# Weight conversion in pairs of pieces, and pooling of batches 2 and 3 by accumulating DMAs, in a fused attention and mixture kernel

## The chip, the cores and the metric

The kernel runs on one core of one Trainium2 chip. The metric is the device time of one execution, in microseconds (us), as the median of the runs of a measurement. All times below are of the kernel before, unless said otherwise.

## What is computed

Three layers follow one another, all in float32 (cut to what matters):

```python
# attention with pooled keys and values; q, k, v are (4, 8, 576, 64)
k_p = k.reshape(B, H, S // 8, 8, D).mean(axis=3)
v_p = v.reshape(B, H, S // 8, 8, D).mean(axis=3)
attn = softmax(q @ k_p.T / sqrt(D))
x = heads_joined(attn @ v_p)                 # 2304 tokens x 512
# first dense layer; its weights arrive as float64
h = x @ w_in                                 # 512 -> 2048
x = (h * cos(h)) @ w_out                     # 2048 -> 512
# mixture of 8 experts, weighted by a Sinkhorn-normalized gate
P = sinkhorn(exp(x @ w_gate), 8 rounds)
out = sum(P[:, e:e+1] * (relu(x @ w1[e]) @ w2[e]) for e in range(8))
```

## The kernel before

The 2304 tokens are worked in six blocks of 384 (j = 0 to 5). Every float32 product that needs full precision is made of three products of rounded parts: a number is cut into a high part (a copy rounded by ScalarE) and a low part (a subtraction on VectorE or GpSimd, by `halves`).

**Attention** (`attn_weights`, `attn_values`) makes, for each block and each half of the heads, scores on TensorE (`psc`), a maximum, a subtraction, an exponential, row sums and a multiplication with the reciprocals (`at`, in `normalize`), then transposes on TensorE (`ptr`), copies of these (`pt`), and products with the pooled values (`px`), which ScalarE and VectorE cut into `xh` and `xl`. Keys and values must be pooled over eight neighbours first. Batch 0 has its own way, batch 1 is pooled by TensorE (`pk`, `pv` with `band`). For batches 2 and 3, `load_k` and `load_v` load four tiles `kr` and four tiles `vr` each, and `pool_steps` adds each tile's eight parts in three halvings (4, 2, 1 parts); each addition goes to VectorE or GpSimd, as the planner likes. Two ScalarE copies then spread `ks` into `kbd`, which the scores read.

**The first dense layer** runs in two groups of blocks (0 to 3, then 4 and 5) and in four units u of 512 hidden columns. `hidden1` makes `ph` and the cosine (`r`, then `gh` and `gl`), `output1` makes `po` and adds it into `acc`. Its weights are float64. `convert` turns one piece (512 columns) of them into two float32 parts: a 512 KB load (`raw`), an absolute value on ScalarE (`m`), five VectorE operations (L820 to L828: two on `m`, one that joins `m` with the raw words, one that makes `cw`, one that multiplies the low words into it), an addition (`cw`, VectorE or GpSimd), and the two parts `wc` by `halves`. Each part is stored to a scratch tensor `wac` in HBM and, except for u = 0 in the first group, loaded again (`cached`) when TensorE needs it. There are 8 pieces a unit, 32 in all. The pieces of u = 0 are needed within the first microseconds, while attention for blocks 0 to 2 goes on beside them.

**The mixture** takes 48 steps (16 weight units times 3 pairs of blocks); each is a Strassen product with 7 instead of 8 block products (`px`, `py`, `pv` in `first_layer`, `pc`, `qc` in `strassen_layer`).

**What sets the order.** No loop issues instructions directly. Every operation is a node of a graph, with an estimated time for its engine, the tiles it reads and writes, and a latest time (`late`) worked out backwards from goals of TensorE's nodes. `Graph.schedule` then plans: again and again, it takes on each engine the most urgent node that could start first, and emits it. A node with two engines (`VG(n)`: VectorE or GpSimd) goes where it is expected to be done, with some slack. Five queues result: TensorE (PE), ScalarE (ACT), VectorE (DVE), GpSimd (POOL) and SyncE (SP), which issues all DMAs. Each runs its nodes in this order, and an instruction whose input is late holds all that stand behind it on the same engine. Tiles have few slots, and a node that opens a tile waits for the slot. Where the plan sees TensorE idle, `keep_busy` fills in products with the identity matrix (`psc<-ident` and the like, L484), whose result nobody reads. `SHIFTS` is a table of 28 entries (first node, count, by) that moves the latest times of nodes before the planning; its nodes lie in attention, the first dense layer and the first steps of the mixture (node numbers 21 to 2937 of 7773).

Of the kernel before, what the change touches and what calls it, by code (L numbers as in the profile page):

```python
# [20 lines left out]
POOL = 8  # L21
# [31 lines left out]
SHIFTS = (  # L53
# [4 lines left out]
)  # L58
# [59 lines left out]


# [6 lines left out]
class Graph:  # L126

    SIGNAL = {"PE": 0.2, "A": 0.1, "V": 0.1, "G": 0.1, "SP": 0.0}
    HOLD = {"PE": 0.02, "A": 0.2, "V": 0.2, "G": 0.3, "SP": 0.2}

# [114 lines left out]
    def schedule(self, log=None):  # L245
# [28 lines left out]
        while left:  # L274
            best = None
            for e in names:
                found = []
                low = FAR
                for node in ready[e]:
# [7 lines left out]
                    if (e == "G" or (e == "V" and node.port)):  # L287
                        start = max(start, port)
# [104 lines left out]
def pool(n):  # L393
    return 0.24 + n * 0.0022
# [17 lines left out]
def fused_kernel(ctx: ExitStack, tc: tile.TileContext, qT, kT, vT, v0, k1, v1, wa1, wb1, wa2, wb2, wg, out):  # L412
# [33 lines left out]
    k_m, k_cw, k_cs = many(early, "cvm", 2, True), many(early, "cvw", 2, True), many(early, "cvs", 4, True)  # L446
# [110 lines left out]
    def pool_steps(how, r, out, reads_out, n_free):  # L557

        n = POOL // 2
        while n > 1:  # L560
            w = n * n_free
            h = V(w) if how == "V" else VG(w) if how == "VG" else {"engine": "G", "us": pool(w), "port": True}
            tt(h, lambda n=n: r()[:, :n], lambda n=n: r()[:, :n], lambda n=n: r()[:, n:2 * n], ALU.add, [], reads_out[:1])
            n //= 2
        h = V(n_free) if how == "V" else VG(n_free) if how == "VG" else {"engine": "G", "us": pool(n_free), "port": True}
        tt(h, out, lambda: r()[:, 0], lambda: r()[:, 1], ALU.add, reads_out[:1], reads_out[1:])
# [10 lines left out]
    def load_first_k(n, goal):  # L577

        t = buf(xtag[("xh1", "xl1")[n]], [P, 2, POOL, SP], F32, "k0")
        for i in range(2):  # L580
            load(lambda i=i: t[:, i], lambda i=i: kT[:, 0, 2 * n + i], P * POOL * SP * 4, writes=[(t, i)], goal=goal)
        return [(t, i) for i in range(2)]

    def pool_first_k(tiles):
        for hp, (t, i) in enumerate(tiles):
            pool_steps("V", lambda t=t, i=i: t[:, i], lambda t=t, i=i: t[:, i, 0], [(t, i), (t, i)], SP)
# [3 lines left out]
    def load_first_v(goal):  # L590

        tiles = []
        for tag in ("xl2", "xh3", "xl5"):
            t = buf(xtag[tag], [P, 2, DM], F32, "v0")
# [37 lines left out]

    def into_kbd(b, ks, ap, **more):
# [6 lines left out]
    def load_k(b):  # L640
# [15 lines left out]
        for hp in range(HP):  # L656
            kr = buf(k_raw, [P, POOL, SP], F32, "kr")
            load(lambda kr=kr: kr.tile, lambda hp=hp: kT[:, b, hp], P * POOL * SP * 4, writes=[kr], release=250 if b == 3 else 0.0)
            pool_steps("VG", lambda kr=kr: kr.tile, lambda hp=hp: ks[:, hp], [kr, (ks, hp)], SP)
        into_kbd(b, ks, lambda: ks.tile)  # L660

    def load_v(b):
# [4 lines left out]
        for hp in range(HP):  # L667
            vr = buf(k_raw, [SP, POOL, 2 * D], F32, "vr")
            load(lambda vr=vr: vr.tile, lambda hp=hp: vT[:, b - 1, hp], SP * POOL * 2 * D * 4, writes=[vr], release=250 if b == 3 else 0.0)
            pool_steps("VG", lambda vr=vr: vr.tile,  # L670
                       lambda hp=hp: vs[:, 2 * hp:2 * hp + 2, :].rearrange("p h d -> p (h d)"), [vr, (vs, hp)], 2 * D)
# [83 lines left out]
    def x_tiles(j):  # L755
        return tuple(buf(xtag[f"{n}{j}"], [P, KC, NB], F32R, f"{n}{j}") for n in ("xh", "xl"))

    def attn_values(j, half):
# [20 lines left out]
        for hh in range(2):  # L779
# [18 lines left out]
            activate(NB, lambda hp=hp: hi[:, hp, :], px, reads=[bank], writes=[(hi, hp)], from_psum=True)  # L798
            if (j, half) in REST_ON_PE:
                pe(0.19, lambda px=px, hp=hp: nc.tensor.matmul(  # L800
                    out=px(), lhsT=minus.tile, rhs=hi[:, hp, :], start=False, stop=True, skip_group_check=True),
                   [minus, (hi, hp)], [bank], goal=FAR)
                activate(NB, lambda hp=hp: lo[:, hp, :], px, reads=[bank], writes=[(lo, hp)], from_psum=True)
                continue
            tt(V(NB, False), lambda hp=hp: lo[:, hp, :], px,
               lambda hp=hp: hi[:, hp, :].bitcast(F32), ALU.subtract, [bank, (hi, hp)], [(lo, hp)])
# [3 lines left out]
    def convert(u, i, raw=None):  # L810

        if raw is None:
            raw = load_piece(u, i)
# [6 lines left out]
        add("V", one(FU), lambda: v.tensor_scalar(out=mf(), in0=mf(), scalar1=F64_LOW, scalar2=F64_HIGH, op0=ALU.max,  # L820
                                                  op1=ALU.min), [], [m], port=True)
        add("V", one(FU), lambda: v.tensor_scalar(out=m.tile, in0=m.tile, scalar1=3, scalar2=0x3FFFFFFF,
                                                  op0=ALU.logical_shift_left, op1=ALU.bitwise_and), [], [m], port=True)
        add("V", two(FU), lambda: v.scalar_tensor_tensor(out=m.tile, in0=high(), scalar=-2**30, in1=m.tile,
                                                         op0=ALU.bitwise_and, op1=ALU.bitwise_or), [raw], [m], port=True)
        add("V", one(FU), lambda: v.tensor_scalar(out=w.tile.bitcast(I32), in0=m.tile, scalar1=-2**23, scalar2=None,
                                                  op0=ALU.bitwise_and), [m], [w], port=True)
        add("V", two(FU), lambda: v.scalar_tensor_tensor(out=w.tile, in0=low(), scalar=2.0**-52, in1=w.tile, op0=ALU.mult,  # L828
                                                         op1=ALU.mult), [raw], [w], port=True)
        tt(VG(FU), lambda: w.tile, mf, lambda: w.tile, ALU.add, [m], [w])  # L830
        parts = [buf(k_w if u == 0 else k_cs, [P, FU], F32R, "wc") for _ in range(2)]
# [587 lines left out]
```

## Time and profile before

| what | value |
|---|---|
| median of 3 runs | 1937.77 us (1937.17 to 1937.92) |
| span of the profiled execution, first to last instruction | 1935.3 us |
| median less that span | 2.5 us |
| TensorE busy in the span | 1920.6 us (99%), 13056 products |
| VectorE, ScalarE, GpSimd busy | 1497.4, 1080.9, 385.2 us |
| granted TensorE clock | 0.999 of full speed |
| DMA traffic | 392.89 MB, 203 GB/s on average |

The profile is of one execution. Its own device time is not given apart from the span, so sums are made against the span, and the 2.5 us by which the median is longer are carried along. Products on TensorE overlap, so its busy time says that it had work, not that it ran at its peak; the waits of TensorE are what it lost entirely. Times within the span count from its first instruction.

### The profile page before, as it was taken

The numbers are of one execution on the slowest core, as the hardware profiler recorded it, in microseconds if no ns is written. First come the engines' busy times: TensorE is split into PE (matmuls) and PEld (weight loads), VectorE is DVE, ScalarE is ACT, GpSimd is POOL, SyncE is SP. The second block draws the span as 40 slices with busy tenths as digits, with TensorE's granted clock in tenths as the row PEclk, the third lists the DMA queues.
The fourth block names the chain that finished last, engine by engine and source line by source line (L and its number), as shares of the span: only waits on it lengthen the run. The fifth ranks groups of instructions, "written<-read, shape, count | busy, mean of one in ns | idle before, by whom it ended". The sixth has DMA issues, their size and how long they took to land.

```text
span 1935.3 us, 34165 instructions
## 1 busy us (share of the span) xinstructions
PE 1920.6 (99%) x13056; PEld 1887.3 (98%) x13056; DVE 1497.4 (77%) x2783; ACT 1080.9 (56%) x2318; POOL 385.2 (20%) x317
## 2 busy tenths in 40 slices
PE   9999999999999999999999999999999999999999
PEld 7799999899999999999999999999999999999998
DVE  8997887855787777777787787777777877877776
ACT  5664545743556665555556555555555565555553
POOL 2523343310102021212112021212121120212120
PEclk9999999999999999999999999999999999999999
DMA  8465566443465646546546455455465464554552
GB/s 296 143 193 183 190 219 243 164 152 104 176 226 225 230 180 238 212 180 235 211 176 261 170 229 228 185 234 211 182 234 211 176 261 169 229 227 183 227 215 112
DMA packets 102020, 392.89 MB, mean 203 GB/s; under 512 B 11360, under 2 KB 16096, under 8 KB 101856
## 3 DMA queue, kind: packets, MB, share of 16 engines
q1 hardware_dynamic: 101856, 390.71, 54.2%
q8 instruction: 103, 1.69, 0.4%
q14 instruction: 61, 0.50, 0.1%
HBM read 352.65 MB, written 38.01 MB: 202 GB/s over the span
## 4 chain that ended last, share of the span: by engine, by line
PE 96%; DVE 3%; ACT 0%; issue 0%; DMA 0%; SPq 0%; POOL 0%; DVEq 0%; POOLq 0%; ACTq 0%
PE pc L1282 21%; PE qc L1282 16%; PE py L1187 16%; PE px L1187 10%; PE pv L1187 10%; PE po L862 3%; PE po L864 3%; PE po L863 3%; PE ph L862 3%; PE ph L863 3%; PE ph L864 3%; DVE at L512 1%; PE psc L684 1%; PE px L787 1%; PE ptr L773 1%
## 5 line engine op out<-in xcount | busy, mean ns | idle before, releaser
L1282 PE MATMUL pc<-vhi,gl 128*128 128x256 f32 x1152 | 322.8, 280 | 0.0
L1282 PE MATMUL pc<-vlo,gh 128*128 128x256 f32 x1152 | 322.7, 280 | 0.0
L1282 PE MATMUL pc<-vhi,gh 128*128 128x256 f32 x1152 | 322.0, 280 | 0.0
L1187 PE MATMUL py<-xc,whi 128*128 128x384 f32 x1152 | 295.1, 337 | 0.8 <-DVE c L512 0.8
L512 DVE TENSOR_TENSOR gl<-sf,gh 128x384 fp32r<-128x384 f32 x384 | 229.9, 627 | 31.0 <-ACT gh L495 30.9
L495 ACT ACTIVATE gh<-sf 128x384 fp32r<-128x384 f32 x384 | 194.3, 522 | 92.5 <-DVE sf L512 90.4
L1282 PE MATMUL qc<-vhi,gh 128*128 128x256 f32 x864 | 243.8, 282 | 0.5 <-DVE qc L512 0.5
L512 POOL TENSOR_TENSOR raw<-raw 128x512 f32<-128x512 f32 x44 | 57.2, 1301 | 938.0 <-DVE wlo L512 530.9
L1282 PE MATMUL qc<-vhi,gl 128*128 128x256 f32 x864 | 242.4, 281 | 0.0
L1282 PE MATMUL qc<-vlo,gh 128*128 128x256 f32 x864 | 241.5, 279 | 0.0
L1282 PEld LDWEIGHTS pc<-vhi,gl 128*128 128x128 f32 x1152 | 216.7, 188 | 0.0
L1282 PEld LDWEIGHTS pc<-vhi,gh 128*128 128x128 f32 x1152 | 216.4, 188 | 0.0
L1282 PEld LDWEIGHTS pc<-vlo,gh 128*128 128x128 f32 x1152 | 216.4, 188 | 0.0
L1187 PEld LDWEIGHTS py<-xc,whi 128*128 128x128 f32 x1152 | 200.6, 188 | 1.8 <-DVE c L512 1.1
L1187 PE MATMUL px<-xc,whi 128*128 128x384 f32 x768 | 197.7, 338 | 0.0
L1187 PE MATMUL pv<-xc,whi 128*128 128x384 f32 x768 | 196.7, 337 | 0.0
L1187 PE MATMUL py<-xc,wlo 128*128 128x384 f32 x576 | 193.7, 336 | 0.0
L1282 PEld LDWEIGHTS qc<-vhi,gh 128*128 128x128 f32 x864 | 162.3, 188 | 2.5 <-DVE qc L512 0.9
L1282 PEld LDWEIGHTS qc<-vlo,gh 128*128 128x128 f32 x864 | 162.4, 188 | 0.0
L1282 PEld LDWEIGHTS qc<-vhi,gl 128*128 128x128 f32 x864 | 162.3, 188 | 0.0
L862 PE MATMUL ph<-xh,wc 128*128 128x384 f32 x384 | 132.3, 345 | 1.5 <-DVE r L512 1.5
L862 PE MATMUL po<-gh,wc 128*128 128x384 f32 x384 | 132.5, 345 | 0.0
(173 smaller groups left out, 4619.0 us busy)
## 6 DMA issues: line engine op xcount, KB each, us to landing
xc<-xc SPq DMA_DIRECT2D x350, 768.0 KB, 6.7
wc<-wac SPq DMA_DIRECT2D x112, 256.0 KB, 3.6
raw<-wa SPq DMA_DIRECT2D x48, 512.0 KB, 4.8
raw<-wb SPq DMA_DIRECT2D x48, 512.0 KB, 7.0
wac<-wc SPq DMA_DIRECT2D x64, 256.0 KB, 3.1
out<-acc SPq DMA_DIRECT2D x18, 256.0 KB, 2.0
qc<-qt SPq DMA_DIRECT2D x30, 128.0 KB, 4.0
kr<-kt SPq DMA_DIRECT2D x8, 288.0 KB, 5.0
```

The costliest lines, as they stand in the source:

```text
L495: lambda: nc.scalar.activation(out=out(), in_=in_(), func=func, **{k: v() if callable(v) else v for k, v in more.items()}),
L512: (nc.gpsimd if e == "G" else nc.vector).tensor_tensor(out=out(), in0=in0(), in1=in1(), op=op)
L684: nc.tensor.matmul(out=ps[off:off + n, 2 * hh:2 * hh + 2, :].rearrange("p h s -> p (h s)"), lhsT=qc()[:, hh, off:off + n], rhs=kpool_at[b] ...
L773: nc.tensor.transpose(ps[:, h, :], at[:, i, h, :], ident.tile)
L787: nc.tensor.matmul(out=bank[e * D:(e + 1) * D, off:off + n], lhsT=vs[b][:, 2 * hp + e, :], rhs=pt[:, 2 * hh + e, off:off + n], start=(off ...
L862: nc.tensor.matmul(out=ps, lhsT=lh, rhs=rh, start=(i == 0), stop=False)
L863: nc.tensor.matmul(out=ps, lhsT=lh, rhs=rl, start=False, stop=False)
L864: nc.tensor.matmul(out=ps, lhsT=ll, rhs=rh, start=False, stop=(i == total - 1))
L1187: nc.tensor.matmul(out=ps(), lhsT=l[:, k], rhs=r[:, c, :], start=(start and c + n == 0), stop=(c + n == 3), skip_group_check=True)
L1282: nc.tensor.matmul(out=ps, lhsT=l[:, r], rhs=m[:, k], start=(start and h + n == 0), stop=(h + n == 3), skip_group_check=True)
```

## The change

It has four parts.

1. `convert` works on a pair of pieces: one load of 1 MB, and the operations on 1024 columns, so that 32 chains become 16. For u = 0 the two pieces of a pair are still cut apart into four tiles `wc`. For u = 1 to 3 the parts are written in place, the high one over `m`, the low one over `cw`, and stored by two DMAs of 512 KB; the four tiles kept for parts go away. The two raw slots are now the later places of blocks 4 and 5 of `x` (`Half`).
2. Batches 2 and 3 are pooled by `summed`: SP loads parts 0 and 1 of all heads into one tile `part`, three DMAs issued by GpSimd add the parts 2 and 3, 4 and 5, 6 and 7 into it, and one addition joins the two halves. The inputs are laid out for that on the host side of the interface (`ks`, `vs`).
3. The planner's model: consecutive VectorE and ScalarE instructions are taken to overlap by 0.08 and 0.1 us, GpSimd's DMAs are given a time to landing and 0.9 us of GpSimd, and are taken not to hold the port that VectorE and GpSimd share; nodes that issue such DMAs become urgent 7 us earlier.
4. `SHIFTS` is empty.

```diff
-SHIFTS = (
-    (1245, 20, -1.1), (2934, 4, -1.3), (185, 2, -1.4), (2725, 4, 2.0), (2209, 8, -0.6), (560, 8, -8.3), (91, 4, 1.3),
...
-)
+SHIFTS = ()
...
+    OVERLAP = {"PE": 0.0, "A": 0.1, "V": 0.08, "G": 0.0, "SP": 0.0}
...
-            if node.engine == ("SP",) and node.size:
-                node.late -= 3.0
+            if node.size:
+                node.late -= 3.0 if node.engine == ("SP",) else 7.0
...
-            free[e] = end
+            free[e] = end - self.OVERLAP[e]
...
-            if e == "G" or (e == "V" and node.port):
+            if e == "G" and not node.size or (e == "V" and node.port):
                 port = end
-            if node.size:
+            if node.size and e == "G":
+                dma = max(dma, start + 0.8) + node.size / 300e3
+                end = max(dma, start + 4.0) + 1.5
+            elif node.size:
                 dma = max(dma, start + 0.8) + node.size / 300e3
                 end = dma + 1.5
...
-                s.est = max(s.est, end + (0.0 if same else self.SIGNAL[e] + s.pad))
+                s.est = max(s.est, end + (0.35 * self.OVERLAP[e] if same else self.SIGNAL[e] + s.pad))
...
+    def summed(rows, n, src, out, writes, release=0.0):
+
+        t = buf(k_raw, [rows, 2, n], F32, "part")
+        load(lambda: t.tile, lambda: src()[:, :2], rows * 2 * n * 4, writes=[t], release=release)
+        for j in range(2, POOL, 2):
+            add("G", 0.9, lambda j=j: nc.gpsimd.dma_start(out=t.tile, in_=src()[:, j:j + 2], accum_op=ALU.add), [], [t],
+                size=rows * 4 * n * 4)
+        tt(VG(n), out, lambda: t[:, 0], lambda: t[:, 1], ALU.add, [t], writes)
...
-        for hp in range(HP):
-            kr = buf(k_raw, [P, POOL, SP], F32, "kr")
-            load(lambda kr=kr: kr.tile, lambda hp=hp: kT[:, b, hp], P * POOL * SP * 4, writes=[kr], release=250 if b == 3 else 0.0)
-            pool_steps("VG", lambda kr=kr: kr.tile, lambda hp=hp: ks[:, hp], [kr, (ks, hp)], SP)
+        summed(P, HP * SP, lambda: kS[:, b - 2], lambda: ks.tile.rearrange("p h s -> p (h s)"), [ks], 250.0 if b == 3 else 0.0)
         into_kbd(b, ks, lambda: ks.tile)
...
-        m, w = buf(k_m, [P, FU], I32, "m"), buf(k_cw, [P, FU], F32, "cw")
+        m, w = buf(k_m, [P, 2 * FU], I32, "m"), buf(k_cw, [P, 2 * FU], F32, "cw")
...
-        activate(FU, mf, lambda: high().bitcast(F32), AF.Abs, reads=[raw], writes=[m])
+        activate(2 * FU, mf, lambda: high().bitcast(F32), AF.Abs, reads=[raw], writes=[m])
...
+        if u:
+            t = [lambda: m.tile.bitcast(F32R), lambda: w.tile.bitcast(F32R)]
+            activate(2 * FU, t[0], lambda: w.tile, reads=[w], writes=[m])
+            tt(VG(2 * FU), t[1], lambda: w.tile, lambda: t[0]().bitcast(F32), ALU.subtract, [m], [w])
...
-    FIRST = "kqKqqQQQffvff"
+    FIRST = "kqKqqQQQfvf"
```

How the order moves, at three places. A row gives the line in the kernel, the operation, and the tiles out<-in with the shape.

VectorE at the start, where attention of block 0 is normalized (`sm`, `rs`, then `at<-at,rs`) before its transposes. Before:

```order
L512 TENSOR_TENSOR at<-psc,mx 128x288 x2
L820 TENSOR_SCALAR m<-m 128x512
L822 TENSOR_SCALAR m<-m 128x512
L824 SCALAR_TENSOR_TENSOR m<-raw_186,m 128x512
L703 TENSOR_SCALAR sm_230<-sm_230 128x4
L705 RECIPROCAL rs<-sm_277 128x4
L750 TENSOR_REDUCE sm<-at 128x12
L703 TENSOR_SCALAR sm<-sm 128x12
L705 RECIPROCAL rs<-sm 128x12
L512 TENSOR_TENSOR at<-at,rs 128x288
```

With the change:

```order
L527 TENSOR_TENSOR at<-psc,mx 128x288 x2
L717 TENSOR_SCALAR sm_228<-sm_228 128x4
L719 RECIPROCAL rs<-sm_257 128x4
L527 TENSOR_TENSOR at<-at,rs 128x288
L717 TENSOR_SCALAR sm_269<-sm_269 128x4
L719 RECIPROCAL rs<-sm_269 128x4
L527 TENSOR_TENSOR at<-at,rs 128x288
L837 TENSOR_SCALAR m<-m 128x1024
L839 TENSOR_SCALAR m<-m 128x1024
L841 SCALAR_TENSOR_TENSOR m<-raw_181,m 128x1024
```

The multiplications now stand ahead of the first conversion, and the sum over the second half of the heads (`sm<-at 128x12`) behind it.

GpSimd, where batch 2 is pooled. Before:

```order
L512 TENSOR_TENSOR ks<-kr 128x72
L512 TENSOR_TENSOR gl<-r,gh 128x384 x3
L512 TENSOR_TENSOR kr<-kr 128x288 x2
L512 TENSOR_TENSOR gl<-r,gh 128x384 x2
L512 TENSOR_TENSOR kr<-kr 128x144 x2
L512 TENSOR_TENSOR ks<-kr 128x72 x2
L512 TENSOR_TENSOR vr<-vr 72x512
L512 TENSOR_TENSOR vr<-vr 72x256
L512 TENSOR_TENSOR vs<-vr 72x128
```

With the change:

```order
L527 TENSOR_TENSOR gl<-r,gh 128x384 x2
L650 DMA part<-ks 128x576
L650 DMA part<-vs 72x1024
L650 DMA part<-ks 128x576
L650 DMA part<-vs 72x1024
L650 DMA part<-ks 128x576
L650 DMA part<-vs 72x1024
L527 TENSOR_TENSOR gl<-r,gh 128x384
L527 TENSOR_TENSOR cw<-m,cw 128x1024
L527 TENSOR_TENSOR ks<-part 128x288
L527 TENSOR_TENSOR vs<-part 72x512
```

Additions between the `gl` operations become six DMA issues in a row, the third and the later ones each waiting for the DMA before it on its tile; `gl` and the conversion stand behind them.

ScalarE, where `kbd` of batch 2 is filled (the scores of block 3 read it). Before:

```order
L495 ACTIVATE at<-at 128x864
L503 ACTIVATE acc<-po 128x384
L495 ACTIVATE kbd_154<-ks 64x4x72 x2
L503 ACTIVATE acc<-po 128x384
L495 ACTIVATE at<-at 128x864
```

With the change:

```order
L510 ACTIVATE m<-cw 128x1024
L518 ACTIVATE acc<-po 128x384
L510 ACTIVATE kbd_151<-ks 64x4x72
L510 ACTIVATE r<-ph 128x384
L510 ACTIVATE kbd_151<-ks 64x4x72
L510 ACTIVATE gh<-r 128x384
```

The copies now have the evacuation of a hidden bank (`r<-ph`) directly behind the first of them.

## Rows read from the trace of the kernel before

**Rows 1.** The page: span, busy time of each engine, chain that ended last.

```profile
span 1935.3 us, 34165 instructions
...
PE 1920.6 (99%) x13056; PEld 1887.3 (98%) x13056; DVE 1497.4 (77%) x2783; ACT 1080.9 (56%) x2318; POOL 385.2 (20%) x317
...
PE 96%; DVE 3%; ACT 0%; issue 0%; DMA 0%; SPq 0%; POOL 0%; DVEq 0%; POOLq 0%; ACTq 0%
```

**Rows 2.** Busy time by stretch: start:end, length, busy (xcount) of each engine.

```profile
13.50:80.30 66.80, 62.31 (x403) 49.70 (x404) 63.15 (x124) 42.52 (x82) 28.19 (x30) 1.00 0.73 242
58.00:76.00 18.00, 14.02 (x84) 12.91 (x83) 16.88 (x29) 10.76 (x21) 9.05 (x10) 1.00 0.54 176
76.00:125.00 49.00, 48.87 (x298) 42.41 (x297) 47.71 (x96) 34.03 (x61) 18.27 (x17) 1.00 0.45 144
125.00:350.00 225.00, 225.00 (x1322) 220.73 (x1321) 186.19 (x334) 117.96 (x224) 80.06 (x72) 1.00 0.61 207
530.00:1930.00 1400.00, 1399.73 (x9965) 1397.66 (x9963) 1081.24 (x2014) 790.47 (x1750) 226.03 (x165) 1.00 0.54 209
```

**Rows 3.** Waits of PE over the span: what waited for whom, us, times, longest.

```profile
PE ph L484 <- ACT r L495: 1.7, 1, 1.7
PE ph L862 <- DVE r L512: 1.5, 1, 1.5
PE psc L484 <- DVE at L512: 1.5, 1, 1.5
PE py L1187 <- DVE c L512: 0.8, 1, 0.8
PE po L864 <- DVE wc L512: 0.8, 1, 0.8
PE ptr L773 <- DVE sm L703: 0.7, 1, 0.7
```

**Rows 4.** Timeline of PE: start, us, engine, line, operation, tiles, count, idle before.

```profile
13.64 4.51 PE L484 MATMUL psc<-ident 128*128 128x128 f32 x38 [1.52 <-DVE at L512]
17.99 0.60 PE L773 MATMUL ptr<-ident,at 128*72 128x128 f32 x4
...
66.57 1.38 PE L484 MATMUL ph<-ident 128*128 128x128 f32 x10 [1.66 <-ACT r L495]
...
81.16 1.19 PE L773 MATMUL ptr<-ident,at 128*72 128x128 f32 x8
```

**Rows 5.** Timeline of DVE, the same columns.

```profile
13.51 0.42 DVE L820 TENSOR_SCALAR m<-m 128x512 f32<-128x512 f32 x1
...
14.42 0.69 DVE L824 SCALAR_TENSOR_TENSOR m<-raw,m 128x512 int32<-128x512 int32 x1
...
17.07 0.40 DVE L512 TENSOR_TENSOR at<-at,rs 128x288 f32<-128x288 f32 x1
...
25.50 0.56 DVE L512 TENSOR_TENSOR xl<-px,xh 128x384 fp32r<-128x384 f32 x1 [0.65 <-ACT xh L495]
...
80.36 1.30 DVE L512 TENSOR_TENSOR at<-at,rs 128x288 f32<-128x288 f32 x2
...
83.42 3.78 DVE L512 TENSOR_TENSOR at<-at,rs 128x288 f32<-128x288 f32 x3
```

**Rows 6.** Timeline of POOL, the same columns.

```profile
20.20 1.51 POOL L512 TENSOR_TENSOR wc<-cw,wc 128x512 fp32r<-128x512 f32 x1 [3.34 <-ACT wc L495]
...
32.58 1.27 POOL L512 TENSOR_TENSOR cw<-m,cw 128x512 f32<-128x512 f32 x1 [5.04 <-DVE cw L828]
...
82.66 4.22 POOL L512 TENSOR_TENSOR vr<-vr 72x512 f32<-72x512 f32 x3
```

**Rows 7.** Timeline of ACT, the same columns.

```profile
76.97 0.89 ACT L495 ACTIVATE kbd<-ks 64x288 f32<-64x288 f32 x2
```

**Rows 8.** DMA issues: tiles, queue, operation, count, KB each, median us to landing.

```profile
raw<-wb SPq DMA_DIRECT2D x48, 512.0 KB, 7.0
kr<-kt SPq DMA_DIRECT2D x8, 288.0 KB, 5.0
```

More of the change, by code (lines that the diff above doesn't have):

```diff
@@ L117, in __getitem__, with part, __init__ @@
         return self.tile[key]
+    def part(self, n):
+        return self, n
+class Half:
+    def __init__(self, buf, k):
+        self.buf, self.k = buf, k
+    def __getitem__(self, key):
+        return self.buf.tile[:, self.k][key]
+    def part(self, n):
+        return self.buf, (self.k, n)
 class Node:
@@ L411, in fused_kernel @@
 @with_exitstack
[L412 removed]
+def fused_kernel(ctx: ExitStack, tc: tile.TileContext, qT, kT, kS, vS, v0, k1, v1, wa1, wb1, wa2, wb2, wg, out):
     nc = tc.nc
@@ L666, in load_v @@
         vs = buf(k_vs, [SP, H, D], F32, "vs")
[L667 to L671, printed above, removed]
+        summed(SP, DM, lambda: vS[:, b - 2], lambda: vs.tile.rearrange("p h d -> p (h d)"), [vs], 250.0 if b == 3 else 0.0)
         vpool[b] = vs
@@ L824, in convert @@
[L824 to L829, printed above, removed]
@@ L830, in convert @@
-        tt(VG(FU), lambda: w.tile, mf, lambda: w.tile, ALU.add, [m], [w])
-        parts = [buf(k_w if u == 0 else k_cs, [P, FU], F32R, "wc") for _ in range(2)]
-        halves(FU, lambda: w.tile, w, lambda k: parts[k].tile, parts)
-        for k in range(2):
-            load(lambda k=k: wac[u, i, k], lambda k=k: parts[k].tile.bitcast(F32), P * FU * 4, reads=[parts[k]],
-                 writes=[kept_wa[u, i, k]])
-        return parts
+        activate(2 * FU, mf, lambda: high().bitcast(F32), AF.Abs, reads=[raw], writes=[m])
@@ new lines, in convert @@
+        add("V", one(2 * FU), lambda: v.tensor_scalar(out=mf(), in0=mf(), scalar1=F64_LOW, scalar2=F64_HIGH, op0=ALU.max,
+                                                      op1=ALU.min), [], [m], port=True)
+        add("V", one(2 * FU), lambda: v.tensor_scalar(out=m.tile, in0=m.tile, scalar1=3, scalar2=0x3FFFFFFF,
+                                                      op0=ALU.logical_shift_left, op1=ALU.bitwise_and), [], [m], port=True)
+        add("V", two(2 * FU), lambda: v.scalar_tensor_tensor(out=m.tile, in0=high(), scalar=-2**30, in1=m.tile,
+                                                             op0=ALU.bitwise_and, op1=ALU.bitwise_or), [raw], [m], port=True)
@@ new lines, in convert @@
+        add("V", one(2 * FU), lambda: v.tensor_scalar(out=w.tile.bitcast(I32), in0=m.tile, scalar1=-2**23, scalar2=None,
+                                                      op0=ALU.bitwise_and), [m], [w], port=True)
+        add("V", two(2 * FU), lambda: v.scalar_tensor_tensor(out=w.tile, in0=low(), scalar=2.0**-52, in1=w.tile, op0=ALU.mult,
+                                                             op1=ALU.mult), [raw], [w], port=True)
+        tt(VG(2 * FU), lambda: w.tile, mf, lambda: w.tile, ALU.add, [m], [w])
@@ new lines, in convert @@
+        pieces = (2 * n, 2 * n + 1)
+        if u:
+            t = [lambda: m.tile.bitcast(F32R), lambda: w.tile.bitcast(F32R)]
+            activate(2 * FU, t[0], lambda: w.tile, reads=[w], writes=[m])
+            tt(VG(2 * FU), t[1], lambda: w.tile, lambda: t[0]().bitcast(F32), ALU.subtract, [m], [w])
+            for k, b in enumerate((m, w)):
+                load(lambda k=k: wac[u, 2 * n:2 * n + 2, k].rearrange("i p n -> p i n"),
+                     lambda b=b: b.tile.bitcast(F32).rearrange("p (i n) -> p i n", i=2), P * 2 * FU * 4, reads=[b],
+                     writes=[kept_wa[u, i, k] for i in pieces])
+            return None
@@ new lines, in convert @@
+        out = []
+        for c, i in enumerate(pieces):
+            parts = [buf(k_w, [P, FU], F32R, "wc") for _ in range(2)]
+            halves(FU, lambda c=c: w[:, c * FU:(c + 1) * FU], w, lambda k, parts=parts: parts[k].tile, parts)
+            for k in range(2):
+                load(lambda i=i, k=k: wac[u, i, k], lambda k=k, parts=parts: parts[k].tile.bitcast(F32), P * FU * 4, reads=[parts[k]],
+                     writes=[kept_wa[u, i, k]])
+            out.append(parts)
+        return out
@@ L948, in fused_kernel @@
                 if u == 0:
-                    for i in range(2 * FC):
-                        weights[i] = convert(0, i, raws[i] if i < len(raws) else None)
-                else:
-                    for i in range(2 * FC):
-                        convert(u, i)
+                    for n in range(FC):
+                        weights[2 * n], weights[2 * n + 1] = convert(0, n, raws[n] if n < len(raws) else None)
+                else:
+                    for n in range(FC):
+                        convert(u, n)
                     for i in range(2 * FC):
```

71 lines of the change are left out of this document (35 added, 36 removed), and 3 rows, old and new, of the table SHIFTS.

## The prediction

> **What bounds the kernel now.** I read the page first, then a table of stretches, then the waits of TensorE, and last the timelines around those waits.
>
> The page [rows 1] says that TensorE is busy for 1920.6 of 1935.3 us and that 96% of the chain that ended last is its own work. The change takes none of that work away: both orders hold the same products, apart from products with the identity matrix, of which 25 instead of 35 are issued. So only the time that TensorE loses can be won, and that is little. The stretches [rows 2] show where: from 125 to 350 us and from 530 to 1930 us TensorE is busy all the time but for 0.3 us, between 76 and 125 us it lacks 0.13 us, and between 58 and 76 us it lacks 4 us of 18. The list of its waits [rows 3] gives the causes: 1.5, 1.7, 1.5 and 0.8 us before 76 us, where VectorE or ScalarE was late, 0.7 us at transposes in the attention of the last blocks, and 0.8 us where the mixture begins. Some time is hidden in identity products: 38 records ran from 13.64 to 17.99 us, ahead of the first transposes, and 10 from 66.57 us [rows 4]. So up to 76 us the work ahead of TensorE sets the time; after that TensorE does.
>
> Who is late there? From 13.5 to 80.3 us VectorE was busy for 63.15 of 66.8 us [rows 2]; it is the bound of the first 80 us. Part of that busy time is no work: a multiplication triple took 3.78 us while GpSimd's pooling `vr` ran for 4.22 us [rows 5, 6], though one multiplication takes 0.40 us [rows 5], so 2.6 us were waiting for the other engine.
>
> **The change, step by step.** I take one place of TensorE's program as the mark: the first transposes of block 2, which began at 81.16 us [rows 4]. In both orders the same work stands ahead of it: 96 products of `hidden1`, 45 of `output1`, 48 transposes, 28 of `px`, 20 of `pk`, 10 of `pv`, and 38 instead of 40 of scores. Whoever comes to the mark earlier ends earlier by as much, since almost nothing was lost behind it [rows 2].
>
> *Start.* Before, three conversion operations and a sum over a whole half stood between the last subtraction and the last multiplication that the first transposes need; the conversions began at 13.51 us, that multiplication at 17.07 us [rows 5]. Now the multiplications come first: about 1.4 us of small operations and two multiplications of 0.40 us, and the transposes can start near 15.0 us instead of 17.99 us [rows 4]. This is no gain by itself, since VectorE begins its conversions 1.4 us later, at 14.9 us. The first weight part was complete at 21.7 us before (20.20 plus 1.51) [rows 6]; now it takes five operations at 1024 columns (4.5 us), an addition on GpSimd (1.27 us at 512 columns [rows 6], some 2.5 us at twice that), 0.6 us on ScalarE and 1.3 us on GpSimd, so about 24 us. The order has TensorE's first hidden products near 24 us too, ahead of the pooling of batch 1, so I cost that at nothing beyond the order.
>
> *VectorE's list up to the mark.* The two queues hold these instructions from the first conversion to the multiplication that the mark waits for. Before: 8 pieces, 24 operations of one input at 0.43 us from start to start, 16 of two inputs at 0.67, 11 additions and subtractions at 0.61 [rows 5]: 27.7 us; with 90 others 59.6 us. Now: 5 pairs, two of whose pieces are already of u = 1. The trace has no such width. By 128x384 at 0.56 and 128x512 at 0.69 us [rows 5] a two-input operation gains 1 ns a column, so 1.2 us at 1024; a one-input one lies between 0.42 us (nothing more) and 0.84 us (double), and I take 0.71, since the instruction's fixed part is paid once. So 15 at 0.71, 10 at 1.2, two additions at 1.14 and four at 0.61: 27.4 us, with 78 others 57.9 us. VectorE's list is 1.7 us shorter, 1.4 us of which its later begin takes back: 0.3 us.
>
> *VectorE's blocked time.* Before, it took from 13.51 to 81.66 us (80.36 plus 1.30) [rows 5] for 59.6 us of work, so 8.5 us were spent blocked or idle, beside 28.19 us of GpSimd's work [rows 2]. GpSimd's list up to there shrinks to about 22 us: the additions of `kr` and `vr` go; one of `ks` and one of `vs` remain, and 1024-wide ones replace pairs. At the same share 8.5 us become 6.6: 1.9 us less.
>
> So the mark comes 2.2 us earlier, at 79 us. The bounds: if VectorE were never late, TensorE would need 57.6 us of its own work from 15.0 us and stand there at 72.6 us, 8.6 us earlier; if the blocked time stayed and GpSimd's six DMA issues cost VectorE as much as a `vs` addition each, it would be 1.5 us later. I take 2.2, since TensorE and VectorE run in step there and the sums leave TensorE waiting for nothing else.
>
> *Behind the mark.* The remaining 11 pairs save VectorE some 0.8 us each, and batch 3's pooling goes too. TensorE waits for none of it [rows 2], so this is worth nothing. The two later waits, 0.7 and 0.8 us [rows 3], lie where the order is now another; they may go, or double: I take half, 0.8 us, with 1.5 us either way.
>
> *Queues.* SP issues 16 loads of 1 MB instead of 32 of 512 KB, 40 stores instead of 64, 4 loads of `part` instead of 16 of `kr` and `vr`. GpSimd issues 12 DMAs. A 512 KB load landed in 7.0 us [rows 8]; pairs come later by a few us, and the first of them is issued where two single ones were, so I cost it at nothing; if that cover fails, the first hidden products wait, which is inside the upper bound.
>
> *End and steady part.* The last operations on all engines stand in the same order; nothing changes there.
>
> Sum: 2.2 + 0.8 = 3.0 us less than the span of 1935.3, so 1932.3. The median is 2.5 us above that span, so **1934.8 us**. About 0.2%, 3.9 us, is what a measurement of this kernel can tell from no change, so "faster" begins below 1933.9 and "slower" above 1941.6.
>
> **A wait that is added.** The three accumulating DMAs of a tile run one after another, and on GpSimd everything behind them waits: `gl`, an addition of the conversion, `ks`; then, on ScalarE, `kbd` with the hidden banks `r<-ph` behind it. No row shows such a DMA. The nearest is a load of the same 288 KB on SP's queue, 5.0 us to landing [rows 8]. The first can start near 50 us, when the slots of batch 1's rows are free; three of 5.0 us, 0.7 for `ks` and 0.9 for `kbd` end near 67 us. Before, `kbd` was done at 77.9 us [rows 7]. So there are 10 us of cover, and each of the three may take 8 us before anything is late. That is why I cost it at nothing.
>
> The Trainium skill speaks against this step: SBUF — State Buffer, section "SBUF: two separate sides", says that a DMA from GpSimd's queue has its descriptors written by GpSimd's cores, which are locked out while VectorE runs an operation that takes both ports, and gives 620 ns that became about 3100. By that, an estimate from the page, three links would be 7.5 us later, still covered; six in a row 15 us, and the sum would be about 1939. No row here shows a DMA from that queue; that the two engines block each other, the 3.78 us triple does show [rows 5, 6].
>
> **Rivals.**
> - *VectorE's lag goes almost altogether.* For it: VectorE does 10 pieces instead of 8 up to the mark and still has the shorter list, and the new order has fewer identity products. Against: it was busy for 95% of that stretch [rows 2], and still would be. With four to eight of the 8.6 us won, and the later waits gone: 1928 to 1933, 1930 in the middle. Chance 0.17.
> - *Slower: the accumulating DMAs come late.* It decides where one takes over 8 us from issue to landing. At 12 us the chain ends at 88 us, 10 us after 77.9; ScalarE stands at `kbd`, hidden banks aren't emptied, and TensorE stops: 1935 plus 10, so 1945. For it: GpSimd issues in order, and VectorE is nearly always busy. Against: 288 KB landed in 5.0 us [rows 8]. Chance 0.10.
> - *Slower: the late part without the table.* The waits of 0.7 and 0.8 us [rows 3] grow to several us each where attention for blocks 4 and 5 and the gate run beside full queues: with 7 us more, 1942. Against it: VectorE has slack there and everything behind 530 us runs with TensorE full [rows 2]. Chance 0.08.
> - *Nothing moves.* What was won at the start is given back, because the first pairs' weights come late: 1937 to 1938. Chance 0.05.
>
> **How the numbers follow.** The forecast's case has 0.60 and its own range is 1931.5 to 1938.5; 0.23 of it falls below 1933.9. Faster by over 0.2%: 0.23 + 0.17 = 0.40. Within: 0.37 + 0.05 = 0.42. Slower: 0.10 + 0.08 = 0.18. The range of 1929 to 1941 leaves out the fastest end of the first rival and most of the two slower ones, not quite 2 in 10.
>
> **What would show it.** In the profile after: the first transposes near 15 us; the first hidden products near 25 us; the transposes of block 2 near 79 us (72.6 would make the first rival right, over 81 the change's point wrong); waits of TensorE under 4 us in all before 125 us; GpSimd's DMAs landing within 8 us and `kbd<-ks` before 78 us; VectorE at 1024 columns near 0.7 and 1.2 us. A TensorE that waits for `kbd`, for `gl` or for `r` behind GpSimd's DMAs would make it wrong.

## The result, and the profile after

The changed kernel took 1961.68 us (median of 4 runs, 1958.98 to 1963.71) beside 1937.58 us for the kernel before. The ratio is 1.0122, with an interval of 1.0108 to 1.0137: 24 us slower. The profiled execution took 1958.98 us, the least of the four; its span is 22 us longer than before. The forecast was 1934.8 us, and its range ended at 1941.

Busy time by stretch of the changed kernel, with the columns of [rows 2] and one stretch more:

```profile
13.50:80.30 66.80, 62.96 (x396) 50.23 (x397) 63.08 (x109) 48.60 (x80) 25.56 (x21) 0.97 0.87 267
58.00:76.00 18.00, 17.52 (x113) 16.35 (x112) 17.27 (x31) 13.77 (x25) 7.30 (x7) 1.00 0.97 249
76.00:125.00 49.00, 47.33 (x287) 41.04 (x286) 46.92 (x85) 35.90 (x59) 8.53 (x8) 1.00 0.48 158
...
530.00:1930.00 1400.00, 1384.07 (x9783) 1373.03 (x9782) 1074.95 (x1990) 786.35 (x1728) 212.45 (x151) 1.00 0.55 208
700.00:1930.00 1230.00, 1214.16 (x8579) 1204.08 (x8578) 944.69 (x1714) 675.46 (x1492) 189.86 (x135) 1.00 0.55 206
```

Between 58 and 76 us TensorE lacks 0.5 us instead of 4; this is the stretch in which the change was to win its time. The loss is in the mixture: in the 1400 us from 530 to 1930 us TensorE lacks 15.9 us instead of 0.3, and gets through 9783 products instead of 9965. The waits of TensorE over the span (what waited for what: us, times, longest) name two places:

```profile
PE qc L1313 <- DVE qc L527: 11.4, 14, 0.8
PE py L1218 <- DVE pv L527: 4.9, 14, 0.4
...
PE px L499 <- ACT xh L510: 1.9, 1, 1.9
```

In the kernel before, nothing waited for `pv`, and `qc` was waited for once, behind 1900 us:

```profile
PE qc L1282 <- DVE qc L512: 0.5, 1, 0.5
```

One such wait of 0.5 us stands at the end of the changed kernel too; the other 13 of `qc` and the 14 of `pv`, 27 in all, are new. Each of the two comes back every 90 us, once in a unit of three steps. To part the two halves of the program, I use the first product of the mixture's second layer (`pc`) and the last product. Timeline of TensorE, first before, then after:

```profile
525.47 0.28 PE L1282 MATMUL pc<-vhi,gh 128*128 128x256 f32 x1
...
1930.91 0.28 PE L1282 MATMUL qc<-vhi,gl 128*128 128x256 f32 x1
```

```profile
15.85 1.04 PE L790 MATMUL ptr<-ident,at 128*72 128x128 f32 x8
...
78.74 1.03 PE L790 MATMUL ptr<-ident,at 128*72 128x128 f32 x8
...
524.32 0.28 PE L1313 MATMUL pc<-vhi,gh 128*128 128x256 f32 x1
...
1953.02 0.28 PE L1313 MATMUL qc<-vhi,gl 128*128 128x256 f32 x1
```

The transposes of block 2, my mark, begin at 78.74 us (81.16 before [rows 4]; forecast: 79). The second layer begins at 524.32 instead of 525.47, still 1.15 us ahead. From there to the last product it is 1428.70 us instead of 1405.44: 23.26 us lost in the steady part, about 1.7 us in each of 14 units. Taken together, 23.26 less 1.15 are the 22 us of the span.

What happens there is seen where the same products follow one another in both kernels: `py`, `px`, `qc`, `pv`. In the kernel before, VectorE, GpSimd and TensorE (start, us, engine, line, operation, tiles, count, idle before):

```profile
1026.44 0.68 DVE L512 TENSOR_TENSOR wlo<-raw,whi 128x512 fp32r<-128x512 f32 x1
1027.04 0.75 DVE L1269 SCALAR_TENSOR_TENSOR acc<-pc,pr,acc 128x512 f32<-128x512 f32 x1
1027.70 0.42 DVE L512 TENSOR_TENSOR qc<-qc,t 128x256 f32<-128x256 f32 x1
1028.04 1.36 DVE L512 TENSOR_TENSOR gl<-sf,gh 128x384 fp32r<-128x384 f32 x1
1029.32 0.55 DVE L512 TENSOR_TENSOR gl<-spare,gh 128x384 fp32r<-128x384 f32 x1
...
1027.69 1.30 POOL L512 TENSOR_TENSOR wlo<-raw,whi 128x512 fp32r<-128x512 f32 x1 [1.87 <-ACT whi L495]
...
1028.58 0.34 PE L1187 MATMUL px<-xc,wlo 128*128 128x384 f32 x1
1028.75 0.28 PE L1282 MATMUL qc<-vhi,gh 128*128 128x256 f32 x1
```

In the changed kernel:

```profile
1031.54 0.68 DVE L527 TENSOR_TENSOR wlo<-raw,whi 128x512 fp32r<-128x512 f32 x1
1032.13 1.65 DVE L527 TENSOR_TENSOR gl<-sf,gh 128x384 fp32r<-128x384 f32 x1
1033.71 0.74 DVE L1300 SCALAR_TENSOR_TENSOR acc<-pc,pr,acc 128x512 f32<-128x512 f32 x1
1034.37 0.42 DVE L527 TENSOR_TENSOR qc<-qc,t 128x256 f32<-128x256 f32 x1
...
1031.63 1.74 POOL L527 TENSOR_TENSOR wlo<-raw,whi 128x512 fp32r<-128x512 f32 x1 [0.71 <-ACT whi L510]
...
1033.66 0.34 PE L1218 MATMUL px<-xc,wlo 128*128 128x384 f32 x1
1034.84 0.38 PE L1313 MATMUL qc<-vhi,gh 128*128 128x256 f32 x1 [0.84 <-DVE qc L527]
```

Before, `qc<-qc,t` ended at 1028.12 us, 0.6 us ahead of the product that needs it, and the `gl` behind it was the one that GpSimd held up (1.36 us instead of 0.55). Now one `gl` stands ahead of `acc` and `qc`, and GpSimd's `wlo` runs beside it: it takes 1.65 us, and TensorE waits. By these rows it takes both: the `gl` alone, about 0.5 us from start to start, would have fitted into the 0.6 us to spare; the 1.1 us that it is held do not. The other place, in the changed kernel:

```profile
1067.12 1.65 DVE L527 TENSOR_TENSOR gl<-spare,gh 128x384 fp32r<-128x384 f32 x1
...
1069.62 0.55 DVE L527 TENSOR_TENSOR pv<-py,s 128x384 f32<-128x384 f32 x1
...
1066.87 1.47 POOL L527 TENSOR_TENSOR raw<-raw,raw 128x512 f32<-128x512 f32 x1 [0.94 <-DVE raw L527]
...
1070.23 0.61 PE L1218 MATMUL py<-xc,whi 128*128 128x384 f32 x2 [0.35 <-DVE pv L527]
```

Here `pv<-py` is late behind a `gl` of 1.65 us, beside a GpSimd operation of 1.47 us. So both kernels have such holds; what changed is which work stands behind one.

### The profile page after: what moved, and what is told of

Read it like the earlier page. It is cut to its first block, busy times and chain, and to the rows that moved or that the text cites. A ratio compares the mean times of both kernels' runs of the same rounds, so it can differ in the third digit from the quotient of the medians.

```text
span 1957.3 us, 33817 instructions
## 1 busy us (share of the span) xinstructions
PE 1927.5 (98%) x13036; PEld 1884.9 (96%) x13036; DVE 1489.9 (76%) x2709; ACT 1088.3 (56%) x2296; POOL 330.6 (17%) x249
## 4 chain that ended last, share of the span: by engine, by line
PE 89%; DVE 8%; issue 2%; ACT 1%; DMA 0%; POOL 0%; ACTq 0%; POOLq 0%
PE pc L1313 19%; PE qc L1313 15%; PE py L1218 14%; PE pv L1218 9%; PE px L1218 9%; PE po L893 3%; PE po L895 3%; PE po L894 3%; PE ph L893 3%; PE ph L894 3%; PE ph L895 3%; DVE gl L527 2%; PE psc L698 1%; DVE acc L1300 1%; DVE raw L527 0%
## 5 line engine op out<-in xcount | busy, mean ns | idle before, releaser
L527 DVE TENSOR_TENSOR gl<-sf,gh 128x384 fp32r<-128x384 f32 x384 | 250.8, 676 | 30.6 <-ACT gh L510 30.4
L527 POOL TENSOR_TENSOR raw<-raw 128x512 f32<-128x512 f32 x32 | 41.9, 1308 | 1025.6 <-DVE wlo L527 616.9
L1313 PEld LDWEIGHTS qc<-vhi,gh 128*128 128x128 f32 x864 | 162.4, 188 | 20.0 <-DVE qc L527 15.9
L510 ACT ACTIVATE qc<-pc 128x256 f32<-128x256 f32 x144 | 53.0, 368 | 175.6 <-PE pc L1313 175.2
L1218 PEld LDWEIGHTS px<-xc,whi 128*128 128x128 f32 x768 | 132.8, 188 | 0.0
```

Of the source, the lines that this page charges most:

```text
L510: lambda: nc.scalar.activation(out=out(), in_=in_(), func=func, **{k: v() if callable(v) else v for k, v in more.items()}),
L527: (nc.gpsimd if e == "G" else nc.vector).tensor_tensor(out=out(), in0=in0(), in1=in1(), op=op)
L1218: nc.tensor.matmul(out=ps(), lhsT=l[:, k], rhs=r[:, c, :], start=(start and c + n == 0), stop=(c + n == 3), skip_group_check=True)
L1313: nc.tensor.matmul(out=ps, lhsT=l[:, r], rhs=m[:, k], start=(start and h + n == 0), stop=(h + n == 3), skip_group_check=True)
```

## Experiments

Each run has a base of the kernel before on the same chip. "Second layer" is the start of the first `pc` product and the time from there to the last product, in the profiled execution, which is one of those behind the median and not always near it (c_gpsimd_off's took 1950.3 us, c_gpsimd_on_vector's 1955.4).

| run | median us | ratio, interval | second layer: start, length us |
|---|---|---|---|
| kernel before | 1937.6 | | 525.5, 1405.4 |
| change | 1961.7 | 1.0122, 1.0108 to 1.0137 | 524.3, 1428.7 |
| c_no_overlap | 1942.2 | 1.0024, 1.0014 to 1.0033 | 530.2, 1405.8 |
| b_overlap_only | 1965.5 | 1.0142, 1.0125 to 1.0159 | 530.8, 1429.1 |
| c_overlap_early | 1936.9 | 0.9999, 0.9989 to 1.0008 | 524.6, 1406.1 |
| c_scalar_overlap | 1952.5 | 1.0077, 1.0062 to 1.0092 | 532.4, 1414.6 |
| c_vector_overlap | 1954.3 | 1.0085, 1.0070 to 1.0100 | 528.7, 1418.1 |
| c_gpsimd_off | 1944.4 | 1.0035, 1.0022 to 1.0049 | 530.0, 1414.3 |
| c_gpsimd_on_vector | 1951.2 | 1.0067, 1.0050 to 1.0084 | 529.1, 1420.4 |
| c_vector_planned | 1936.7 | 0.9997, 0.9988 to 1.0007 | 524.3, 1406.4 |
| b_no_table | 1940.9 | 1.0022, 1.0012 to 1.0031 | 529.1, 1405.9 |
| e_neither | 1941.2 | 1.0017, 1.0007 to 1.0026 | 529.3, 1406.5 |
| e_pairs | 1938.9 | 1.0004, 0.9995 to 1.0013 | 527.6, 1406.5 |
| e_pool | 1939.8 | 1.0009, 0.9999 to 1.0018 | 525.9, 1406.5 |

### Which part of the change did it

My theory after the result: the overlaps that the planner now counts (part 3) changed the order in the mixture. The rival: the new tiles and transfers, or the empty table.

```diff
-    OVERLAP = {"PE": 0.0, "A": 0.1, "V": 0.08, "G": 0.0, "SP": 0.0}
+    OVERLAP = {"PE": 0.0, "A": 0.0, "V": 0.0, "G": 0.0, "SP": 0.0}
```

> The changed kernel with the planner's overlaps set to zero, all else as changed. Theory 1 (the overlaps alone changed the order of the mixture): between 700 and 1930 us no wait of TensorE for `qc` or `pv`, and 1934 to 1938 us. Theory 2 (the new tiles and transfers of pairs and pooling, or the empty table of shifts, leave the mixture in the worse order): 28 waits as before the edit, 1959 to 1963 us.

The kernel before, with that part alone:

```diff
+    OVERLAP = {"PE": 0.0, "A": 0.1, "V": 0.08, "G": 0.0, "SP": 0.0}
...
-            free[e] = end
+            free[e] = end - self.OVERLAP[e]
...
-                s.est = max(s.est, end + (0.0 if same else self.SIGNAL[e] + s.pad))
+                s.est = max(s.est, end + (0.35 * self.OVERLAP[e] if same else self.SIGNAL[e] + s.pad))
```

> The kernel before with the planner's overlaps added (0.1 us on ScalarE, 0.08 us on VectorE), nothing else; table, single pieces and pooling by additions stay. Theory 1: the mixture falls into the order of the changed kernel, 13 to 15 waits each for `qc` (0.84 us) and `pv` (0.35 us), and the time is 22 to 25 us over the kernel before: 1959 to 1963 us. Theory 2: 1936 to 1940 us and no such waits.

The changed kernel with the overlaps up to the mixture:

```diff
+        early = {id(n) for n in self.nodes[:self.mixture]}
...
-            free[e] = end - self.OVERLAP[e]
+            lap = self.OVERLAP[e] if id(node) in early else 0.0
+            free[e] = end - lap
...
+    g.mixture = len(g.nodes)
```

> The changed kernel with the overlaps counted only for the nodes ahead of the mixture's 48 steps. Theory 1: the mixture is as before, and the 1.2 us by which the changed kernel was ahead at 700 us stays: 1935 to 1937.5 us. Theory 2: 1959 to 1963 us. Beside the run without overlaps it shows what the overlaps are worth ahead of the mixture: 0 to 2 us by the lead at 700 us.

The stretch from 700 us without overlaps, and the first two waits of the kernel before with them alone:

```profile
700.00:1930.00 1230.00, 1230.00 (x8747) 1228.37 (x8747) 949.91 (x1729) 684.68 (x1525) 205.43 (x150) 1.00 0.54 208
```

```profile
PE qc L1283 <- DVE qc L513: 11.3, 14, 0.8
PE py L1188 <- DVE pv L513: 4.9, 14, 0.4
```

Without the overlaps TensorE is busy for all of the 1230 us; with them alone, single pieces, additions and the old table notwithstanding, the same waits appear and the second layer takes 1429.1 us. That settles it for the first theory. But two times missed what I had set. With the overlaps alone it came to 1965.5 us, over the 1963: there the second layer starts 5.3 us later than in the kernel before. Without overlaps it came to 1942.2 us, over the 1938: the second layer starts 5.9 us later than in the change. Counted ahead of the mixture only, the overlaps give 1936.9 us. So in the changed kernel the same two numbers are worth 5.3 us ahead of the mixture, where I had expected 0 to 2, and cost 23 us in it; in the kernel before they cost time in both halves.

### One count or both

```diff
-    OVERLAP = {"PE": 0.0, "A": 0.1, "V": 0.08, "G": 0.0, "SP": 0.0}
+    OVERLAP = {"PE": 0.0, "A": 0.1, "V": 0.0, "G": 0.0, "SP": 0.0}
```

> The changed kernel with an overlap counted for ScalarE alone (0.1 us; VectorE's is zero). Theory S (it is ScalarE's count that brings GpSimd's operation in front of the late VectorE operation): the 28 waits in the mixture stay, and 1958 to 1967 us, since ahead of the mixture the run without overlaps was up to 5 us later. Theory V (it is VectorE's count): no waits, 1936 to 1943 us.

> The changed kernel with an overlap counted for VectorE alone (0.08 us; ScalarE's is zero). Theory V: the 28 waits stay, 1958 to 1967 us. Theory S: no waits, 1936 to 1943 us. Where both runs wait, either count is enough; where neither does, only the two together do it.

Neither theory fits. Waits from 700 to 1930 us, ScalarE's count alone, then VectorE's alone:

```profile
PE py L1218 <- DVE pv L527: 5.5, 14, 0.4
```

```profile
PE py L1218 <- DVE pv L527: 3.0, 14, 0.3
```

Either count alone makes one of the two waits and lengthens the second layer by 9 and 13 us; together they make both. (With VectorE's count `qc` comes late too, but by 0.16 us a time, counted from one product's start to the next, which the trace doesn't book as idle.) So it is no one bad value, but an order that hangs on small numbers. Why the planner puts a `gl` ahead of `qc` when it takes VectorE for free 0.08 us earlier was not followed through its arithmetic and stays open.

### Is it GpSimd's hold

In the changed kernel, with every operation at its place in the plan, GpSimd's work in the mixture goes to ScalarE, as copies that leave out its subtractions and additions, then to VectorE, with nothing left out. The edit of the first (the second has "V" in place of "A"):

```diff
-            node.run(e) if len(node.engine) > 1 else node.run()
+            to = "A" if e == "G" and id(node) in steady else e
+            node.run(to) if len(node.engine) > 1 else node.run()
```

> The changed kernel, planned alike, but every operation that GpSimd has in the mixture's 48 steps is issued as a copy on ScalarE at the same place in the order; this leaves out the subtractions and additions of those weight pieces. Theory A (VectorE is late because GpSimd's operation holds it for 1.1 us just before): nearly all of the 28 waits go, 1936 to 1942 us. Theory B (VectorE's new order is late by itself, or the matmuls' order is): the waits stay, 1955 us or more.

> The changed kernel, planned alike, but every operation that GpSimd has in the mixture's 48 steps is issued on VectorE at the same place in the order; nothing is left out. Theory A (the hold by GpSimd, 1.1 us in front of each late operation): in its place VectorE has 0.6 us more work, so each wait gets some 0.5 us shorter: those of 0.35 us go, those of 0.84 us go to 0.3 or 0.4, and the time is 1942 to 1952 us. Theory B (VectorE's order is late by itself): VectorE has 81 us more work between 700 and 1930 us, waits grow, 1962 us or more.

Then with the planner told that this work is VectorE's:

```diff
 def VG(n):
+    if ALONE:
+        return V(n)
     return {"engine": ("V", "G"), "us": (two(n), pool(n)), "port": True}
...
+    ALONE.append(True)
```

> The changed kernel with overlaps counted everywhere, but in the mixture's 48 steps the weight pieces' additions and subtractions are VectorE's alone already in the plan, so that GpSimd has nothing there and TensorE's order is planned with it. Theory A (the holds by GpSimd, which the plan places badly when it counts overlaps): no waits of 0.3 us or more for `qc` or `pv` in the mixture, although VectorE has some 90 us more work there; 1936 to 1942 us, and with the lead of 1.2 us at 700 us kept, the likeliest is 1937. Theory C (counting overlaps makes the plan too tight for any VectorE order): 14 waits or more of 0.2 us and over, 1945 us or more.

From 700 to 1930 us: the stretch with ScalarE, the wait with VectorE, the stretch with VectorE in the plan:

```profile
700.00:1930.00 1230.00, 1227.52 (x8691) 1218.62 (x8690) 894.71 (x1735) 743.23 (x1656) 0.00 (x0) 1.00 0.55 208
```

```profile
PE qc L1315 <- DVE qc L529: 4.4, 13, 0.3
```

```profile
700.00:1930.00 1230.00, 1229.48 (x8753) 1225.86 (x8751) 973.69 (x1880) 687.71 (x1514) 0.00 (x0) 1.00 0.55 207
```

With no GpSimd beside it the 27 waits are gone, though VectorE's and TensorE's orders are those of the change. The median of this run, 1944.4 us, is over the 1942 that I had set, and 9 us of the 23 stay in its second layer. They lie at another place, the products `py` behind `pv`, which start 0.25 us late in each unit (1.4 us in one), right behind ScalarE's `py<-px`; ScalarE works without a gap there, and one of the added copies stands just ahead (L530):

```profile
889.39 0.63 ACT L530 ACTIVATE vlo<-raw 128x512 fp32r<-128x512 f32 x1
...
890.86 0.47 ACT L512 ACTIVATE py<-px 128x384 f32<-128x384 f32 x1
...
891.39 0.62 PE L1223 MATMUL py<-xc,whi 128*128 128x384 f32 x2
```

With 0.6 us of its own work in place of the 1.1 us hold, VectorE leaves 13 waits of 0.3 us, as theory A says; the second layer is still 15 us longer than before, of which, counted from start to start of the products, about 8 us lie at these 13. Planned for VectorE alone, the mixture has neither wait, but for the one of 0.5 us at the end, and takes 1406.4 us, although VectorE is busy 29 us longer in the stretch than in the change. In the changed order the hold is the cause; the order decides whether it counts. That version (1936.7 us) and the one with overlaps ahead of the mixture (1936.9 us) are the best here, and neither can be told from the kernel before.

### What the forecast's own terms were worth

The table emptied in the kernel before:

```diff
-SHIFTS = (
...
-)
+SHIFTS = ()
```

> The kernel before with the table of shifts emptied, nothing else. If the table is worth something ahead of the mixture, this is slower by it: 1938 to 1946 us (no overlap, pairs and pooling by DMA came to 1942.2 us together with the empty table). If it is worth nothing, 1937 to 1939 us. In neither case does the mixture wait for `qc` or `pv`.

Then pairs and pooling apart, with an empty table and overlaps ahead of the mixture in all three. The first has neither; the second has pairs and the additions of `kr` and `vr`; the third has single pieces and `summed`.

```diff
-        summed(P, HP * SP, lambda: kS[:, b - 2], lambda: ks.tile.rearrange("p h s -> p (h s)"), [ks], 250.0 if b == 3 else 0.0)
+        for hp in range(HP):
+            kr = buf(k_raw, [P, POOL, SP], F32, "kr")
...
+            pool_steps(lambda kr=kr: kr.tile, lambda hp=hp: ks[:, hp], [kr, (ks, hp)], SP, VG)
```

> The kernel before with the empty table and with overlaps counted only ahead of the mixture: single pieces, pooling by additions. It is the base of the two runs after it and stands against the changed kernel with overlaps ahead of the mixture alone (1936.9 us). By the prediction's terms (pairs and pooling by DMA save 2 us ahead of block 2's transposes): 1938 to 1941 us, transposes of block 2 at 80 to 82 us. By the rival that the order the planner happens on decides, and not the work saved: anything from 1934 to 1946 us.

> As the changed kernel with overlaps ahead of the mixture alone, but batches 2 and 3 pooled by additions as before. By the prediction's terms the pairs alone shorten VectorE's list by about a microsecond and leave GpSimd's additions: 1937 to 1939 us. By the rival of the order: 1934 to 1946 us, with no regard to the work saved.

> The kernel before with the empty table, overlaps ahead of the mixture alone, and batches 2 and 3 pooled by accumulating DMAs; weights converted in single pieces. By the prediction's terms it saves the additions of `kr` and `vr` and thus about 1.5 us of VectorE's blocked time: 1936.5 to 1939 us. By the rival of the order: 1934 to 1946 us.

The empty table costs 3.8 us (1940.9 against 1937.2 on that chip), and all of it behind my mark. In that run's profiled execution the transposes of block 2, with as many products ahead of them as before, begin 2.0 us earlier than before, and the second layer 3.6 us later:

```profile
79.14 1.03 PE L768 MATMUL ptr<-ident,at 128*72 128x128 f32 x8
...
529.05 0.28 PE L1277 MATMUL pc<-vhi,gh 128*128 128x256 f32 x1
```

From the empty table, with overlaps ahead of the mixture, pairs save 2.3 us (1941.2 to 1938.9), pooling by DMA 1.4 us (to 1939.8), both 4.3 us (to 1936.9, from another group of runs): nearly the sum, but twice the 2.2 us of the terms, since pairs saved more than the 1 us expected. Two of the three times lie just over the ranges that the terms gave (1941.2 over 1941, 1939.8 over 1939), and in the run with neither of the two the mark came at 83.85 us, not at 80 to 82. Without overlaps the two together save nothing (1940.9 to 1942.2). So the terms hold in one planner's order and are lost in another; the rival of the order is not refuted by them.

## Why the prediction was wrong

*What bounds the kernel* was right, and so were VectorE's prices. VectorE's operations at 1024 columns up to 350 us (busy, mean ns):

```profile
L845 DVE SCALAR_TENSOR_TENSOR cw<-raw,cw 128x1024 f32<-128x1024 uint32 x16 | 20.1, 1261 | 0.2
L841 DVE SCALAR_TENSOR_TENSOR m<-raw,m 128x1024 int32<-128x1024 int32 x16 | 19.5, 1220 | 0.2
L837 DVE TENSOR_SCALAR m<-m 128x1024 f32<-128x1024 f32 x16 | 13.3, 830 | 0.2 <-ACT m L510 0.2
...
L839 DVE TENSOR_SCALAR m<-m 128x1024 int32<-128x1024 int32 x16 | 11.1, 693 | 0.1
```

Two-input ones took 1.22 and 1.26 us (forecast 1.2), one-input ones 0.69 to 0.83 (0.71).

*Start and mark.* The first transposes began at 15.85 us (forecast 15.0), those of block 2 at 78.74 (79). The first hidden products were forecast near 24 to 25 us; they came at 29.1 us, and had come at 31.3 before: I had taken the first finished weight part for all that they need, but they need `xl` too, which VectorE finished at 27.9 us. I had forecast under 4 us of waits ahead of 125 us; TensorE's waits there add up to 8.3 us, and were 7.9 before (2.1 of each at the very start, a wait that [rows 3] leaves out), with 50 fill records instead of 70.

*Behind the mark.* I gave the later waits 0.8 us more of a gain. Instead the lead shrank from 2.4 to 1.15 us: between 76 and 125 us TensorE lacks 1.7 us, which were 0.1 [rows 2]. The sum up to 525 us was thus 1.2 us where 3.0 were forecast. The rule behind it, that whoever comes to the mark earlier ends earlier by as much, did not hold in other runs either: c_overlap_early, whose mixture has neither wait, begins block 2's transposes at 78.28 us, 2.9 us ahead, and the second layer 0.9 us ahead; the empty table alone turned 2.0 us ahead into 3.6 us behind. So even with the mixture put right the 3.0 us did not come: 1936.9 us against 1937.8, not told from no change. That TensorE had lost almost nothing behind the mark in the old order did not say what it would lose there in a new one.

*The accumulating DMAs* were rightly costed at nothing, by less than I thought. GpSimd's issues for `ks` of batch 2 (three for `vs` stand between them), the sum, and ScalarE's `kbd`:

```profile
54.52 1.02 POOL L650 DMA_DIRECT2D part<-ks  x1
...
59.60 0.89 POOL L650 DMA_DIRECT2D part<-ks  x1 [2.83 <-DMA part<-ks]
...
67.60 0.89 POOL L650 DMA_DIRECT2D part<-ks  x1 [4.63 <-DMA part<-ks]
...
75.51 0.81 POOL L527 TENSOR_TENSOR ks<-part 128x288 f32<-128x288 f32 x1
...
76.92 0.43 ACT L510 ACTIVATE kbd<-ks 64x288 f32<-64x288 f32 x1
77.93 0.44 ACT L510 ACTIVATE kbd<-ks 64x288 f32<-64x288 f32 x1
```

GpSimd's twelve accumulating DMAs landed after 4.5 to 8.5 us each (forecast: 5.0, and late over 8), and `kbd` was done at 78.4 us, not 67; before it was done at 77.9 [rows 7]. The cover of 10 us was used up, but TensorE has no wait for `kbd`. The Trainium skill's rule that I had set against this step (SBUF — State Buffer, "SBUF: two separate sides") is neither borne out nor refuted: a load of the same size by SP took 4.5 us, but adding into the tile and being held up aren't told apart here. (My sum for six such links should have read 1939.8 us, with 10 of 15 us covered, and not about 1939.)

*The step that failed* is "End and steady part. The last operations on all engines stand in the same order; nothing changes there." I had looked at the last operations, found them alike, and taken the 48 steps ahead of them to be so too. The change's third part, the overlaps, thus got no price of its own, though the planner's numbers act on every node of the plan, those of the mixture too. The runs put it at 23 us in the mixture, and none of my rivals held it. The nearest, the late part without its table, names a loss that the runs do show, but not this one: with the table alone emptied, 5.6 us go between the mark and the second layer, while the mixture takes 1405.9 us.

## What to carry to other kernels

A planner's constant is an edit to every stage: compare the order of the steady loop, place by place, and not its end alone, since what is lost there is lost once a round. Where VectorE empties banks just in time, look in the trace for GpSimd's operations beside it, and ask what stands behind each hold; an engine that is 76% busy with slack on average can still be late 27 times. And try the parts of a change apart before judging any: here the pairs and the pooling saved 4.3 us (with overlaps ahead of the mixture), the empty table cost 3.8, and the overlaps cost 23 in the mixture.

## What the runs showed of the hardware

*A wait costs TensorE more than its idle time.* The waits of TensorE are not all that it loses, as I had put it ahead of the prediction. The 27 new waits add up to 15.8 us, the second layer grew by 23.3: 0.28 us more for each. The rows show most of it: from the last `px` product to `qc` it is 1.18 us where 0.17 is usual, 1.0 us lost with 0.84 booked as idle, because the product ahead is booked for 0.34 us; and the next product follows after 0.22 us (1035.06) instead of 0.12. Counted like that, from start to start, the 13 waits at `qc` cost 14.4 us and the 14 at `py` 8.6, 23.0 together. By the Trainium skill (TensorE: Matmul & The Clock Gate, "Step-by-step: what each phase is for") a product's end overlaps the start of the next; that a broken stream loses this overlap agrees with these rows.

*The hold works both ways.* VectorE's `gl` took 1.65 us instead of 0.55 beside GpSimd's `wlo`; and this `wlo` took 1.74 us instead of 1.30, since VectorE's own `wlo`, begun at 1031.54, ran until 1032.22. Each held the other in turn. The Trainium skill (SBUF — State Buffer, "SBUF: two separate sides") says that the engine that starts first has the shared ports for its whole instruction; these rows agree, with 0.44 us for the one and 1.1 us for the other.

*The granted clock fell once, at the start.* In the changed kernel:

```profile
22.00:26.00 4.00, 2.06 (x16) 1.39 (x13) 3.93 (x6) 1.91 (x4) 3.26 (x3) 0.96 0.97 332
26.00:30.00 4.00, 3.37 (x17) 2.81 (x17) 3.90 (x7) 1.19 (x2) 0.45 (x1) 0.61 0.65 237
```

After a stretch in which TensorE was busy for 2.06 of 4 us it was granted 0.61 of full speed, so mostly the lower level of 1.2 GHz; eight transposes, begun at 27.52 us, took 1.82 us there instead of 1.04. In the kernel before, TensorE was busy for 3.91 us from 22 to 26 us, and the clock stayed at 1.00.

*The first 500 us vary more than the rest.* Four profiled executions with the same planned order ahead of the mixture (the change, c_vector_planned, c_gpsimd_on_vector, c_gpsimd_off) began the second layer at 524.3, 524.3, 529.1 and 530.0 us, while the eight lengths under 1407 us in the table lie between 1405.4 and 1406.5. So the parts above are compared by medians, and what is said of one execution's start of the second layer is known to no better than this.
